# Attention block on one core: one of two integer adds goes from VectorE to GpSimd, a third PSUM bank for VectorE's tiles, and a changed planner

## The chip, the cores and the metric

The kernel runs on one core of one Trainium2 chip. The metric is device time in microseconds (us), the median of several executions. The engines are TensorE (PE), VectorE (DVE), ScalarE (ACT), GpSimd (POOL) and SyncE (SP), which issues most DMAs. Matmul results go to PSUM, in banks of 128 x 512 fp32.

## The reference

```python
# x (1, 2048, 448), wqkv (448, 1344), wo (448, 448), all bf16; 16 heads of 28
qkv = (x @ wqkv).reshape(B, S, 3, H, Dh).transpose(2, 0, 3, 1, 4)
q, k, v = qkv[0], qkv[1], qkv[2]
scores = jnp.einsum("bhqd,bhkd->bhqk", q, k) * (Dh ** -0.5)
p = softmax(scores, axis=-1)
o = jnp.einsum("bhqk,bhkd->bhqd", p, v)
return o.transpose(0, 2, 1, 3).reshape(B, S, D) @ wo
```

## The kernel before

The 16 heads form 4 groups of 4, and the 2048 queries form 4 blocks of 512. A group and a query block make a "set"; there are 16. In a set each of the 4 heads has 16 key tiles of 128 keys, so the whole run has 16 x 4 x 16 = 1024 score tiles of 128 keys x 512 queries. Scores are computed with keys on the partitions. A head uses 32 rows or columns of TensorE, so up to four heads' matmuls run side by side.

Each score tile must go through an exponential and then be multiplied with V. There are two ways:

- On ACT: `do_exp` (L802) takes a pair of tiles (128 x 1024, PSUM tag `a0` or `a1`) and writes `pt` in bf16, with its exact exponential.
- On VectorE: `do_a` (L817) converts one tile (128 x 512, PSUM tag `d0` or `d1`) into an int16 number `I` whose bits, read as bf16, approximate the exponential. Up to four tiles of one set make a "chain", kept side by side in one tile `I4` of 128 x 2048. The approximation is improved by using the chain three times with shifted exponents: `do_add` (L840) makes `J1 = I + 43` and `J2 = I + 85`, both 128 x 2048 int16 in SBUF, and the three are multiplied with V, V x 201/256 and V x 159/256 (tiles `VA`, `VS`), all into the same accumulator.

So a tile on ACT costs one output matmul on PE and a tile on VectorE costs three. `emit_s` (L621) issues the score matmuls; `do_pv` (L900) issues the output matmuls in waves of four heads, normally two waves in a row, into the PSUM bank `o`. The last column of V's tile is a one, so that the sums of the softmax come out with the output. At the end of a set `finish_set` copies `o` out, sends the sums through DMAs to get their reciprocals spread over the partitions, and multiplies.

Between these stand the "jobs" of PE: projections of K, Q and V for later groups (`k_job`, `q_job`, `v_job`, L230 and L445), bounds for the exponent (`kn_job`, `qn_job`), and the output projection (`oproj_job`, L481). They all use the PSUM bank `m`. Where PE has nothing to do, it multiplies zeros (`dense`, L651 and L654).

The order is made by a planner inside the kernel, while the program is built. It keeps an estimated time for each engine (`free`), a time for each event (`evt`) and for each PSUM bank (`res`), takes the engine that is free first and asks its `pick_...` function what to issue next. The estimated durations are constants such as `D_EXP = 0.912` for a pair on ACT. The estimates decide only the order: on the chip each engine works through its own list in that order and waits on semaphores for its inputs. `pick_pe` puts score matmuls first, then chooses between output matmuls and jobs; `dve_ok` decides whether another tile is given to VectorE, by comparing when the chain would be finished with when ACT would be; `d_banks` lists the banks that are free for such a tile; `pick_dve` orders conversions, adds and the other VectorE work. How many tiles go to ACT and how many to VectorE is therefore a result of the planning. `NCH = 3` chains may be open at once, and each of `I4`, `J1` and `J2` has three buffers.

GpSimd sets constants and loads `wo` at the start and does nothing after that.

Of the kernel before, what the change touches and what calls it, by code (L numbers as in the profile page):

```python
# [16 lines left out]
LAT = 0.2  # L17
# [4 lines left out]
D_EXP = 0.912  # L22
SLOW_V = 1.03
D_SOON = 0.0
S_LEAD = 0.44


class Op:
    def __init__(self, eng, dur, emit, need=(), gives=(), pri=0, acq=None, rel=None, gate=0, lag=0.0, land=0.0,
                 cols=0):  # L30
        self.eng, self.dur, self.emit = eng, dur * (SLOW_V if eng == "DVE" else 1.0), emit
        self.need, self.gives, self.pri = list(need), list(gives), pri
        self.acq, self.rel, self.gate, self.lag, self.land, self.cols = acq, rel, gate, lag, land, cols


@with_exitstack
def kernel(
# [135 lines left out]
        return psum.tile([P, QW], F32, name=tg, tag=tg, bufs=1)  # L173


    free = {"PE": 0.0, "ACT": 0.0, "DVE": 0.0, "SP": 0.0}
    evt = {}
    res = {"a0": 0.0, "a1": 0.0, "d0": 0.0, "d1": 0.0, "o": 0.0, "m": 0.0}
    ops = {"PE": [], "ACT": [], "DVE": [], "SP": []}
# [25 lines left out]
    def run(op, t):  # L205
        op.emit()
        if op.eng == "PE":
            note(t, op.cols)
        end = t + op.dur
        for n in op.gives:  # L210
# [35 lines left out]
    def k_job(g, sc, bank, pri, gate=0, split=2, eng="DVE", epri=None):  # L246
        key = ("K", g, sc)
        n = CC // split

        def mm(part):  # L250
            if part == 0:
                held[key] = bank_tile(bank) if bank[0] != "a" else pair_tile(bank)
            mm_proj(held[key][:, 0:QW], 1, g, sc, range(part * n, (part + 1) * n))

        def evac():
            KAt[(g, sc)] = big.tile([P, QW], BF16, name=f"KA{sc}", tag=f"KA{sc}", bufs=2)
            src = held[key][:, 0:QW]
# [13 lines left out]
        if g == 0:  # L271
            add("ACT", 0.5, lambda: act_square(key, kmask), need=[key + (split - 1,)],
                gives=[("ksq", g, sc)], rel=(bank, 2), pri=pri)
        else:
            add("DVE", 0.34, lambda: square(key, KAt[(g, sc)][:]), need=[key], gives=[("ksq", g, sc)], pri=pri)

    def kn_job(g, bank, pri, gate=0):
        key = ("KN", g)
# [24 lines left out]
        add("DVE", 0.65, spread_rows, need=[("kst", g)], gives=[("km", g)], pri=pri)  # L303

    def kn_first(sc, bank, pri):
        key = ("KN0", sc)
# [27 lines left out]
    def q_job(g, c, bank, pri, gate=0, split=2):  # L334
# [31 lines left out]
        if first:  # L366
            add("ACT", 0.5, lambda: act_square(key, qmask), need=[key + (split - 1,)], gives=[("qsq", g, c)],
                rel=(bank, 2), pri=pri)
        else:
            add("DVE", 0.34, lambda: square(key, QAt[(g, c)][:]), need=[key], gives=[("qsq", g, c)], pri=pri)  # L370
# [30 lines left out]
    def qn_job(g, cs, bank, pri, gate=0):  # L401
# [29 lines left out]
        add("DVE", 1.6, bound, need=[key + (len(cs) - 1,)], gives=[("su",) + key], rel=bank, pri=pri)  # L431
# [32 lines left out]
    def vs_job(h, b, pri):  # L464
# [4 lines left out]

        for k in range(1, NTERM):  # L470
            add("DVE", 0.335, lambda k=k: scale(k), need=[("V", h, XB * b), ("V", h, XB * b + 2)],
                gives=[("VS", h, b, k)], pri=pri + 0.1 * k)

    def oproj_job(c, tq, pri):
        key = ("O", c, tq)
# [185 lines left out]
    def dve_ok(t, k):  # L661
        if chain["cur"] is None and chain["used"] >= NCH:
            return False
        if chain["cur"] is not None and half_left(chain["cur"]["s"], 0) != half_left(chain["cur"]["s"], 1):
            return True
        fin = max(free["DVE"], t + 0.5) + 0.62 * (len(a_fifo) + k + 1) + 1.4 + (1.2 if adds else 0.0)
        return fin <= free["ACT"] + D_EXP * (len(exps) + max(0, left() // 2 - 2)) + 0.2

    def d_banks(t):
        return sorted((b for b in ("d0", "d1") if res[b] is not None and res[b] <= t + D_SOON), key=lambda b: res[b])  # L670

    def d_pick(s, t, acting, taken):
        ch = chain["cur"]
# [159 lines left out]
            chain["cur"] = None  # L833
            adds.append([ch, ch["n"], 1])

    def do_add(t):
        ch, m, k = adds[0]
        w = slice(0, m * QW)
        r = ch[k] = wk.tile([P, HG * QW], I16, name=f"J{k}", bufs=NCH)
        nc.vector.tensor_scalar(out=r[:, w], in0=ch["I"][:, w], scalar1=float(SHIFT[k]), scalar2=None, op0=ALU.add)  # L840
        end = t + (m * QW * 0.00026 + 0.068) * SLOW_V
        for n in range(m):
            pending.append({"step": ch["steps"][n], "k": k, "ap": r[:, n * QW:(n + 1) * QW].bitcast(BF16),
                            "ready": end + LAT, "pt": None, "ch": ch})
        adds[0][2] += 1
        if adds[0][2] == NTERM:
            adds.pop(0)
        return end

    def v_time(e):  # L850
        s, _, j = e["step"]
# [65 lines left out]
    def finish_set(s, end):  # L917
# [37 lines left out]
        add("DVE", 0.26, recip, need=[("den", s)], gives=[("rec", s)], pri=50)  # L955
        add("SP", 0.35, scatter, need=[("rec", s)], gives=[("scr", s)], land=1.1, pri=2)
        add("SP", 0.5, spread, need=[("scr", s)], gives=[("rr", s)], land=5.5, pri=2)
        add("DVE", 0.62, mul, need=[("rr", s)], gives=[("OT", g, c)], pri=60)

    def best(eng, t):  # L960
        b, nxt = None, None
        for op in ops[eng]:
            r = ready(op)
            if r is None:
                continue
            if r <= t:
                if b is None or op.pri < b.pri:
                    b = op
# [8 lines left out]
    def pick_pe(t):  # L977
# [24 lines left out]
            ws = ws[:1]  # L1002
            pv_ok = True
        op_ok = op is not None and t + op.dur <= dl + 0.1
        if pv_ok and (backlog >= 3 or last_chance or not op_ok):
            return do_pv(t, ws), None
        if op_ok:
            return run(op, t), None
# [22 lines left out]
    def pick_dve(t):  # L1031
        flush()
        op, nxt = best("DVE", t)
        if op is None or (op.pri >= 0 and op.gives[0][0] != "V"):
            if adds and adds[0][0]["s"] == cur["oset"] and not any(remain[cur["oset"]]):
                return do_add(t), None
            if a_fifo and a_fifo[0][0] <= t and a_fifo[0][3][0] == cur["oset"] \
                    and not any(remain[cur["oset"]]):
# [7 lines left out]
        if op is not None:  # L1046
            return run(op, t), None
        return None, nmin(nxt, a_fifo[0][0] if a_fifo else None)

    def pick_sp(t):  # L1050
        op, nxt = best("SP", t)
# [1 line left out]
            return run(op, t), None  # L1053
        return None, nxt

    pick = {"PE": pick_pe, "ACT": pick_act, "DVE": pick_dve, "SP": pick_sp}
    stuck = 0
    def late(op):
        return op.gives and op.gives[0][0] == "O" and op.gives[0][1] == CL - 1
# [1 line left out]
    while cur["oset"] < NSET or any(not late(op) for e in ops for op in ops[e]) or any(k[0] == "O" for k in held):  # L1061
# [11 lines left out]
        assert stuck < 4000, (t, cur, left(), pending, [(o.eng, o.need, o.acq) for q in ops.values() for o in q])  # L1073

    s = NSET - 1
    g, c = set_gc(s)
# [95 lines left out]
```

## Time and profile before

| | |
|---|---|
| time, median of 3 runs | 384.09 us (380.04 to 385.84) |
| the profiled execution's own time | 381.23 us |
| its span | 379.2 us |
| granted TensorE clock | 0.999 |
| busy: ACT, PE, DVE, POOL | 359.0, 346.4, 341.9, 20.0 us |
| exponential pairs on ACT | 376 |
| tiles converted on VectorE | 272 |
| adds on VectorE | 136 |
| matmuls of zeros in the program | 58 |

The profile is of one execution. "Busy" is the time in which an engine had an instruction running; for PE the ends of matmuls are modelled. In the lists of groups, a row gives line, engine, operation, output and input tiles, count, then busy time and the mean duration of one, and at last the idle time of the engine just before these instructions, with what ended it. Instructions of one engine overlap slightly, so the mean duration (1183 ns for an exponential pair) is more than busy time divided by count (919 ns). PEld is the loading of weights into TensorE.

### The profile page before, as it was taken

To read this page: it belongs to the slowest core of one execution; us is meant where nothing else is said; L and a number is where in the kernel's file an instruction comes from. 1 tells how busy PE (TensorE), PEld (TensorE's weight loads), DVE (VectorE), ACT (ScalarE), POOL (GpSimd) and SP (SyncE) were. 2 spreads that over 40 slices of the span, in tenths; PEclk is the share of its full clock that TensorE was granted. 3 is DMA by queue.
4 is the path that set the end of the run, shared out by engine and by line. 5 is a ranking of instruction groups with operands and counts; after the bars stand their busy time and mean duration, and the time that the engine had idled before them with its cause. 6 is when DMAs were issued, how large, how long until landed. Compare 5 with 4: busy or idle time off the path is not lost.

```text
span 379.2 us, 8747 instructions
## 1 busy us (share of the span) xinstructions
PE 346.4 (91%) x3442; PEld 113.3 (30%) x3462; DVE 341.9 (90%) x655; ACT 359.0 (95%) x400; POOL 20.0 (5%) x47
## 2 busy tenths in 40 slices
PE   7879999999999999999789999989889899989974
PEld 3443322222333233232222222222222222222222
DVE  2499998999999999999899899899999999999943
ACT  2779999999999999999999999999999999999992
POOL 8830000000000000000000000000000000000000
PEclk9999999999999999999999999999999999999999
DMA  8930001011100000011000001000000011110101
GB/s 251 246 102 16 3 19 38 3 41 28 41 6 15 18 3 29 14 28 40 4 30 7 25 15 41 28 31 2 28 5 4 28 39 42 37 43 12 56 14 48
DMA packets 16082, 14.03 MB, mean 37 GB/s; under 512 B 6077, under 2 KB 13609, under 8 KB 16041
## 3 DMA queue, kind: packets, MB, share of 16 engines
q1 hardware_dynamic: 13704, 11.18, 9.8%
q10 hardware_dynamic: 1824, 1.89, 1.8%
q8 instruction: 27, 0.44, 0.5%
q0 software_dynamic: 512, 0.40, 0.5%
q14 instruction: 15, 0.11, 0.1%
HBM read 7.37 MB, written 1.96 MB: 25 GB/s over the span
## 4 chain that ended last, share of the span: by engine, by line
ACT 56%; PE 22%; issue 9%; DMA 6%; DVE 4%; SPq 2%; ACTq 0%; DVEq 0%
ACT pt L802 54%; PE a L621 9%; PE o L900 6%; PE m L230 3%; DMA rr<-scr 3%; PE m L445 2%; DMA WRAW<-in_wqkv_dram 2%; SPq L359 2%; DVE I L817 1%; DMA QP<-zero 1%; DVE QA L353 1%; DVE J L840 1%; DMA den<-o_sb 1%; ACT sq L244 0%; ACT XT L517 0%
## 5 line engine op out<-in xcount | busy, mean ns | idle before, releaser
L802 ACT ACTIVATE pt<-a 128x1024 bf16<-128x1024 f32 x376 | 345.6, 1183 | 1.5 <-PE d L621 1.1
L817 DVE TENSOR_SCALAR I<-d 128x512 int16<-128x512 f32 x272 | 180.0, 682 | 8.0 <-PE d L621 6.6
L621 PE MATMUL a<-QP,KA 32*128 32x512 bf16 (+1 forms) x742 | 144.9, 380 | 18.2 <-ACT pt L802 17.0
L900 PE MATMUL o<-pt,VA 128*32 128x512 bf16 x752 | 106.5, 385 | 0.5 <-ACT pt L802 0.5
L621 PEld LDWEIGHTS <-KA 32*128 32x128 bf16 (+1 forms) x1024 | 52.6, 91 | 155.8 <-issue 153.6
L621 PE MATMUL d<-QP,KA 32*128 32x512 bf16 x267 | 92.6, 384 | 0.2 <-DVE I L817 0.2
L840 DVE TENSOR_SCALAR J<-I 128x2048 int16<-128x2048 int16 x136 | 90.1, 684 | 0.4
L900 PE MATMUL o<-J,VS 128*32 128x512 bf16 x544 | 74.4, 385 | 0.3
L900 PE MATMUL o<-I,VA 128*32 128x512 bf16 x272 | 65.9, 385 | 0.6 <-issue 0.5
L230 PE MATMUL m<-XT,WRAW 112*32 112x512 bf16 x464 | 35.5, 384 | 0.5 <-ACT XT L517 0.3
L900 PEld LDWEIGHTS <-VA 128*32 128x32 bf16 x1024 | 23.9, 94 | 37.0 <-issue 36.7
L900 PEld LDWEIGHTS <-VS 128*32 128x32 bf16 x544 | 16.5, 94 | 16.4 <-issue 16.4
L445 PE MATMUL m<-WRAW,XT 112*128 112x224 bf16 x112 | 15.4, 261 | 0.0
L230 PEld LDWEIGHTS <-WRAW 112*32 112x32 bf16 x512 | 8.4, 94 | 16.0 <-issue 12.9
L445 PEld LDWEIGHTS <-XT 112*128 112x128 bf16 x128 | 10.2, 97 | 7.8 <-issue 6.3
L262 DVE TENSOR_SCALAR KA<-m,kmask,ones 128x512 bf16<-128x512 f32 x13 | 10.4, 803 | 2.1 <-ACT sq L244 1.9
L353 DVE TENSOR_SCALAR QA<-m,qmask 128x512 bf16<-128x512 f32 x15 | 11.1, 742 | 0.5 <-PE m L230 0.5
L515 DVE COPY XT<-a 112x1024 bf16<-112x1024 bf16 x4 | 2.8, 692 | 9.4 <-ACT XT L517 7.8
L651 PE MATMUL o<-zero 128*128 128x512 bf16 x29 | 10.0, 384 | 1.3 <-issue 1.3
L481 PE MATMUL m<-WO,xs 128*128 128x448 bf16 x36 | 11.0, 359 | 0.0
L951 DVE TENSOR_TENSOR xs<-o_sb,rr 128x512 bf16<-128x512 f32 x12 | 8.2, 683 | 2.5 <-DMA rr<-scr 2.5
L929 DVE COPY o_sb<-o 128x512 f32<-128x512 f32 x15 | 10.3, 685 | 0.1
(104 smaller groups left out, 155.0 us busy)
## 6 DMA issues: line engine op xcount, KB each, us to landing
rr<-scr SPq DMA_DIRECT2D x15, 256.0 KB
QP<-zero SPq DMA_DIRECT2D x16, 128.0 KB
QP<-QA SPq DMA_DIRECT2D x60, 28.0 KB
out_dram<-osb SPq DMA_DIRECT2D x14, 112.0 KB
xs<-in_x_dram SPq DMA_DIRECT2D x3, 448.0 KB
WRAW<-in_wqkv_dram ACTq DMA_DIRECT2D x3, 392.0 KB
QP<-su SPq DMA_DIRECT2D x30, 2.0 KB
xs<-in_x_dram ACTq DMA_DIRECT2D x1, 448.0 KB
```

Source lines behind the costliest of these rows:

```text
L230: nc.tensor.matmul(out=ps[HP * i:HP * (i + 1), :], lhsT=WRAW[t][:, cc, h * Dh:h * Dh + HP], rhs=XT[c][:, cc, :], start=(cc == 0), stop=(cc ...
L262: nc.vector.tensor_scalar(out=KAt[(g, sc)][:], in0=src, scalar1=kmask[:, 0:1], scalar2=ones[:, 0:1], op0=ALU.mult, op1=ALU.add)
L353: nc.vector.tensor_scalar(out=t[:], in0=held[key][:, 0:QW], scalar1=qmask[:, 0:1], scalar2=None, op0=ALU.mult)
L445: nc.tensor.matmul(out=held[key][:, part * w:(part + 1) * w], lhsT=XT[b][:, cc, t * P:(t + 1) * P], rhs=WRAW[2][:, cc, h * w:(h + 1) * w], ...
L481: nc.tensor.matmul(out=held[key][:, 0:D], lhsT=otile(g, c)[:, tq * P:(tq + 1) * P], rhs=WO[:, g, :], start=(g == 0), stop=(g == G - 1))
L621: nc.tensor.matmul(out=out_ap, lhsT=KAt[(g, j // XB)][r, (j % XB) * P:(j % XB + 1) * P], rhs=q[r, :], start=True, stop=True, tile_position ...
L651: nc.tensor.matmul(out=cur["o"][:], lhsT=zero[:, 0:P], rhs=zero[:], start=False, stop=False, skip_group_check=True)
L802: nc.scalar.activation(out=pt[:], in_=ps[:], func=ACT.Exp, scale=LN2 / 128.0)
L817: nc.vector.tensor_scalar(out=dst, in0=pd[:], scalar1=BIAS, scalar2=0.0, op0=ALU.add, op1=ALU.max)
L840: nc.vector.tensor_scalar(out=r[:, w], in0=ch["I"][:, w], scalar1=float(SHIFT[k]), scalar2=None, op0=ALU.add)
L900: nc.tensor.matmul(out=o[HP * i:HP * (i + 1), :], lhsT=vt[:, gg, j % XB, HP * i:HP * (i + 1)], rhs=e["ap"], start=(SETMM[key] == 1), stop= ...
L929: nc.vector.tensor_copy(out=st["o_sb"][:], in_=o[:])
```

## The change

- Of the two adds of a chain, VectorE now makes only `J2 = I + 85`; GpSimd makes `J1 = J2 - 42`, from VectorE's result.
- The planner has a GpSimd engine, with a duration of 2.3 us for such an add (`D_POOL`), and a notion of a port shared by VectorE and GpSimd: VectorE operations marked `port=True`, and its adds, are not planned while a GpSimd add is planned to run, and a GpSimd add is not planned while one of these is.
- `d_banks` may offer the bank `m` as a third bank for a VectorE tile, when fewer than two of `d0` and `d1` are free, fewer than two tiles wait for conversion and no job is about to need `m`.
- `dve_ok` reckons 3.5 us instead of 1.4 us from the last conversion to the end of a chain.
- `pick_pe` lets a job with a priority value below 40 go ahead of waiting output matmuls; `pick_dve` puts adds ahead of conversions; the planner's clock is advanced differently when an engine finds nothing to do.

The diff, cut to its core (the added parameter `port=True` on seven operations with SBUF inputs is left out after the first):

```diff
+D_POOL = 2.3
...
-    free = {"PE": 0.0, "ACT": 0.0, "DVE": 0.0, "SP": 0.0}
+    free = {"PE": 0.0, "ACT": 0.0, "DVE": 0.0, "SP": 0.0, "POOL": 0.0}
     evt = {}
+    port = {"DVE": 0.0, "POOL": 0.0}
+    pool_q = []
...
-            add("DVE", 0.34, lambda: square(key, KAt[(g, sc)][:]), need=[key], gives=[("ksq", g, sc)], pri=pri)
+            add("DVE", 0.34, lambda: square(key, KAt[(g, sc)][:]), need=[key], gives=[("ksq", g, sc)], pri=pri, port=True)
...
-        fin = max(free["DVE"], t + 0.5) + 0.62 * (len(a_fifo) + k + 1) + 1.4 + (1.2 if adds else 0.0)
+        fin = max(free["DVE"], t + 0.5) + 0.62 * (len(a_fifo) + k + 1) + 0.7 + D_POOL + 0.5 + (1.2 if adds else 0.0)
...
     def d_banks(t):
-        return sorted((b for b in ("d0", "d1") if res[b] is not None and res[b] <= t + D_SOON), key=lambda b: res[b])
+        out_ = sorted((b for b in ("d0", "d1") if res[b] is not None and res[b] <= t + D_SOON), key=lambda b: res[b])
+        if len(out_) < 2 and res["m"] is not None and res["m"] <= t and len(a_fifo) < 2:
+            soon = [ready(op) for op in ops["PE"] if op.acq == "m"]
+            if not any(r is not None and r <= t + 1.0 for r in soon):
+                out_.append("m")
+        return out_
...
-    def do_add(t):
-        ch, m, k = adds[0]
+    def add_term(eng, ch, m, k, src, shift, end):
         w = slice(0, m * QW)
         r = ch[k] = wk.tile([P, HG * QW], I16, name=f"J{k}", bufs=NCH)
-        nc.vector.tensor_scalar(out=r[:, w], in0=ch["I"][:, w], scalar1=float(SHIFT[k]), scalar2=None, op0=ALU.add)
-        end = t + (m * QW * 0.00026 + 0.068) * SLOW_V
+        eng.tensor_scalar(out=r[:, w], in0=src[:, w], scalar1=float(shift), scalar2=None, op0=ALU.add)
         for n in range(m):
             pending.append({"step": ch["steps"][n], "k": k, "ap": r[:, n * QW:(n + 1) * QW].bitcast(BF16),
                             "ready": end + LAT, "pt": None, "ch": ch})
-        adds[0][2] += 1
-        if adds[0][2] == NTERM:
-            adds.pop(0)
         return end
 
+    def do_add(t):
+        ch, m, _ = adds.pop(0)
+        end = port["DVE"] = t + (m * QW * 0.00026 + 0.068) * SLOW_V
+        pool_q.append((end + LAT, ch, m))
+        return add_term(nc.vector, ch, m, 2, ch["I"], SHIFT[2], end)
+
+    def pick_pool(t):
+        if not pool_q:
+            return None, None
+        if pool_q[0][0] > t:
+            return None, pool_q[0][0]
+        if port["DVE"] > t:
+            return None, port["DVE"]
+        _, ch, m = pool_q.pop(0)
+        end = port["POOL"] = t + D_POOL * m / HG
+        return add_term(nc.gpsimd, ch, m, 1, ch[2], SHIFT[1] - SHIFT[2], end), None
...
+            if op.port:
+                r = max(r, port["POOL"])
...
-        if pv_ok and (backlog >= 3 or last_chance or not op_ok):
+        if pv_ok and (backlog >= 3 or last_chance or not op_ok) and not (op_ok and op.pri < 40 and pts_used[0] < NPT):
             return do_pv(t, ws), None
...
     def pick_dve(t):
         flush()
         op, nxt = best("DVE", t)
+        can_add = adds and port["POOL"] <= t
+        can_a = a_fifo and a_fifo[0][0] <= t
...
-        if a_fifo and a_fifo[0][0] <= t:
+        if can_add:
+            return do_add(t), None
+        if can_a:
             return do_a(t), None
-        if adds:
-            return do_add(t), None
...
-        cand = nmin(nxt, others if others > t else None)
-        free[e] = max(t + 0.02, cand if cand is not None else t + 0.05)
+        free[e] = max(t + 0.02, nmin(nxt, others))
```

More of the change, by code (lines that the diff above doesn't have):

```diff
@@ L29, in __init__ @@
     def __init__(self, eng, dur, emit, need=(), gives=(), pri=0, acq=None, rel=None, gate=0, lag=0.0, land=0.0,
-                 cols=0):
+                 cols=0, port=False):
         self.eng, self.dur, self.emit = eng, dur * (SLOW_V if eng == "DVE" else 1.0), emit
         self.need, self.gives, self.pri = list(need), list(gives), pri
-        self.acq, self.rel, self.gate, self.lag, self.land, self.cols = acq, rel, gate, lag, land, cols
+        self.acq, self.rel, self.gate, self.lag, self.land, self.cols, self.port = acq, rel, gate, lag, land, cols, port
 @with_exitstack
@@ L173, in bank_tile @@
         return psum.tile([P, QW], F32, name=tg, tag=tg, bufs=1)
-    free = {"PE": 0.0, "ACT": 0.0, "DVE": 0.0, "SP": 0.0}
+    free = {"PE": 0.0, "ACT": 0.0, "DVE": 0.0, "SP": 0.0, "POOL": 0.0}
     evt = {}
+    port = {"DVE": 0.0, "POOL": 0.0}
+    pool_q = []
     res = {"a0": 0.0, "a1": 0.0, "d0": 0.0, "d1": 0.0, "o": 0.0, "m": 0.0}
-    ops = {"PE": [], "ACT": [], "DVE": [], "SP": []}
+    ops = {"PE": [], "ACT": [], "DVE": [], "SP": [], "POOL": []}
     cnt = {"step": 0, "half": 0}
@@ L209, in run @@
         end = t + op.dur
+        if op.port:
+            port["DVE"] = end
         for n in op.gives:
@@ L302, in kn_job @@
         add("DVE", 0.61, red, need=[("KNp", g, NQC - 1)], gives=[("kst", g)], rel=bank, pri=pri)
-        add("DVE", 0.65, spread_rows, need=[("kst", g)], gives=[("km", g)], pri=pri)
+        add("DVE", 0.65, spread_rows, need=[("kst", g)], gives=[("km", g)], pri=pri, port=True)
     def kn_first(sc, bank, pri):
@@ L369, in q_job @@
         else:
-            add("DVE", 0.34, lambda: square(key, QAt[(g, c)][:]), need=[key], gives=[("qsq", g, c)], pri=pri)
+            add("DVE", 0.34, lambda: square(key, QAt[(g, c)][:]), need=[key], gives=[("qsq", g, c)], pri=pri, port=True)
             add("SP", 2.4, rows, need=[key, ("QZ", c, g % 2)] + ([("Oset", ORDER.index((g - 2, c)))] if g > 1 else []),
@@ L430, in qn_job @@
                 acq=bank if k == 0 else None)
-        add("DVE", 1.6, bound, need=[key + (len(cs) - 1,)], gives=[("su",) + key], rel=bank, pri=pri)
+        add("DVE", 1.6, bound, need=[key + (len(cs) - 1,)], gives=[("su",) + key], rel=bank, pri=pri, port=True)
         add("SP", 1.2 * len(cs), place, need=[("su",) + key] + [("QR", g, c) for c in cs],
@@ L471, in vs_job @@
             add("DVE", 0.335, lambda k=k: scale(k), need=[("V", h, XB * b), ("V", h, XB * b + 2)],
-                gives=[("VS", h, b, k)], pri=pri + 0.1 * k)
+                gives=[("VS", h, b, k)], pri=pri + 0.1 * k, port=True)
     def oproj_job(c, tq, pri):
@@ L954, in finish_set @@
         add("SP", 0.6, gather, need=[("osb", s)], gives=[("den", s)], land=1.5, pri=2)
-        add("DVE", 0.26, recip, need=[("den", s)], gives=[("rec", s)], pri=50)
+        add("DVE", 0.26, recip, need=[("den", s)], gives=[("rec", s)], pri=50, port=True)
         add("SP", 0.35, scatter, need=[("rec", s)], gives=[("scr", s)], land=1.1, pri=2)
         add("SP", 0.5, spread, need=[("scr", s)], gives=[("rr", s)], land=5.5, pri=2)
-        add("DVE", 0.62, mul, need=[("rr", s)], gives=[("OT", g, c)], pri=60)
+        add("DVE", 0.62, mul, need=[("rr", s)], gives=[("OT", g, c)], pri=60, port=True)
     def best(eng, t):
@@ L965, in best @@
                 continue
+            if op.port:
+                r = max(r, port["POOL"])
             if r <= t:
@@ L1033, in pick_dve @@
         op, nxt = best("DVE", t)
+        can_add = adds and port["POOL"] <= t
+        can_a = a_fifo and a_fifo[0][0] <= t
         if op is None or (op.pri >= 0 and op.gives[0][0] != "V"):
-            if adds and adds[0][0]["s"] == cur["oset"] and not any(remain[cur["oset"]]):
+            last = not any(remain[cur["oset"]]) if cur["oset"] < NSET else False
+            if can_add and last and adds[0][0]["s"] == cur["oset"]:
                 return do_add(t), None
-            if a_fifo and a_fifo[0][0] <= t and a_fifo[0][3][0] == cur["oset"] \
-                    and not any(remain[cur["oset"]]):
+            if can_a and last and a_fifo[0][3][0] == cur["oset"]:
                 return do_a(t), None
@@ L1041, in pick_dve @@
             return run(op, t), None
-        if a_fifo and a_fifo[0][0] <= t:
+        if can_add:
+            return do_add(t), None
+        if can_a:
             return do_a(t), None
-        if adds:
-            return do_add(t), None
-        if op is not None:
-            return run(op, t), None
-        return None, nmin(nxt, a_fifo[0][0] if a_fifo else None)
+        return None, nmin(nxt, a_fifo[0][0] if a_fifo else None, port["POOL"] if adds else None)
     def pick_sp(t):
@@ L1054, in pick_sp @@
         return None, nxt
-    pick = {"PE": pick_pe, "ACT": pick_act, "DVE": pick_dve, "SP": pick_sp}
+    pick = {"PE": pick_pe, "ACT": pick_act, "DVE": pick_dve, "SP": pick_sp, "POOL": pick_pool}
     stuck = 0
@@ L1069 @@
         others = min(free[n] for n in free if n != e)
-        cand = nmin(nxt, others if others > t else None)
-        free[e] = max(t + 0.02, cand if cand is not None else t + 0.05)
+        free[e] = max(t + 0.02, nmin(nxt, others))
         stuck += 1
-        assert stuck < 4000, (t, cur, left(), pending, [(o.eng, o.need, o.acq) for q in ops.values() for o in q])
+        assert stuck < 40000, (t, cur, left(), pending, [(o.eng, o.need, o.acq) for q in ops.values() for o in q])
     s = NSET - 1
```

## The prediction

> **What bounds the kernel now.** I read the page's busy shares first, then the costliest groups, then each engine's waits, then timelines for the cadence. The page:
>
> ```profile
> span 379.2 us, 8747 instructions
> PE 346.4 (91%) x3442; PEld 113.3 (30%) x3462; DVE 341.9 (90%) x655; ACT 359.0 (95%) x400; POOL 20.0 (5%) x47
> ...
> ACT  2779999999999999999999999999999999999992
> POOL 8830000000000000000000000000000000000000
> ...
> L802 ACT ACTIVATE pt<-a 128x1024 bf16<-128x1024 f32 x376 | 345.6, 1183 | 1.5 <-PE d L621 1.1
> L817 DVE TENSOR_SCALAR I<-d 128x512 int16<-128x512 f32 x272 | 180.0, 682 | 8.0 <-PE d L621 6.6
> L621 PE MATMUL a<-QP,KA 32*128 32x512 bf16 (+1 forms) x742 | 144.9, 380 | 18.2 <-ACT pt L802 17.0
> ...
> L840 DVE TENSOR_SCALAR J<-I 128x2048 int16<-128x2048 int16 x136 | 90.1, 684 | 0.4
> ```
>
> Three engines are above 90%, so the share alone decides nothing. The idle column does. ACT makes 376 exponential pairs (two 128x512 tiles each) and in the whole run waited 1.5 us before them. PE waited 17.0 us for ACT ahead of its score matmuls; VectorE waited 6.6 us for scores. ACT is saturated from 22.8 us (its first exponential in the timeline) until about 369.7 us, and PE and VectorE, though nearly full, follow it. So only fewer exponentials on ACT shorten the main stage: 345.6 / 376 = 0.919 us for each pair taken away. GpSimd (POOL) has nothing after 23.6 us.
>
> **Parts of the change.** I set the instruction lists of the two programs side by side, engine by engine, in program order. Counts before and after:
>
> - ACT: exponential pairs 376 to 364, all else equal. 12 x 0.919 = **-11.0 us** on the engine that sets the end.
> - VectorE: tiles in its own exponential 272 to 296 (265 from the d banks, 31 from the projections' bank m); adds 136 to 74. At 0.662 us each (180.0 / 272 and 90.1 / 136): 24 x 0.662 - 62 x 0.662 = -25.2 us, so 341.9 becomes 316.7, some 86% of the new span. Off the path: nothing from here, but more room.
> - PE: each VectorE tile enters the output product three times instead of once, so 48 matmuls more (pt 752 to 728, I 272 to 296, J 544 to 592). They run four abreast; two waves of four stand 361.83 to 362.37 in the timeline, 0.54 us with the switch, so 12 waves are 2.6 us (0.22 each) to 3.2 (0.27). 18 zero matmuls that only fill gaps go, 0.32 each (257.07 to 257.39): -5.8 us. PE's cover for the shorter span is its 17.0 us of waiting for ACT: 17.0 - 11.0 - 3.2 + 5.8 = 8.6 us are left, plus 40 fillers. Cost nothing; if that cover were gone, a late PE would go to ACT one for one.
> - GpSimd: 74 adds of 128x2048 int16, SBUF to SBUF, each reading the first add's result. The trace has no such operation. The nearest rows:
>
> ```profile
> 1.01 0.29 POOL L133 TENSOR_SCALAR_AFFINE_SELECT ident<-ident 128x128 bf16<-128x128 bf16 x1
> ...
> 3.49 1.03 POOL L161 MEMSET VA<- 128x1024 bf16 x1
> ...
> 11.51 1.67 POOL L163 MEMSET WO<- 128x1792 bf16 x1
> ```
>
> The select reads and writes 128 elements in 287 ns, against 185 ns for one of 128x1: 0.80 ns an element, and 185 + 2047 x 0.80 = 1.83 us for 2048. The memsets, which only write, give (1671 - 1017) / 768 = 0.85 ns, and 1671 + 256 x 0.85 = 1.89 us. If reading and writing each took the memset's rate, one after the other: 1.89 + 2048 x 0.85 = 3.63 us. So 1.83 to 3.63; I take 1.9, as the select both reads and writes at the low rate. As work, 74 x 3.63 = 269 us would still fit; what counts is delay.
>
> The delay: a chain is four tiles, then the first add on VectorE, then GpSimd's, then PE. A product placed too early in PE's fixed order blocks the next score matmuls behind it, and ACT waits for those. From the order I counted, for each of the 74 chains, the score pairs that PE issues between the chain's last tile and its first product with GpSimd's result: 4 pairs in 2 chains, 5 in 12, 6 in 22, 7 in 16, 8 in 17, 9 in 5. A pair lasts 0.911 us (15 exponentials in 13.93 us at 249.18, the last one 1.18 long). The available time is pairs x 0.911 + 0.33 for the score group ahead of the product. The needed time is 0.39 (score) + 0.69 (tile) + 0.60 for each VectorE instruction between (0 to 4, counted chain by chain) + 0.68 (add) + three hand-overs of 0.1 + GpSimd's add. VectorE's 0.60 cadence is read here:
>
> ```profile
> 104.32 0.68 DVE L840 TENSOR_SCALAR J<-I 128x2048 int16<-128x2048 int16 x1
> 104.91 0.68 DVE L817 TENSOR_SCALAR I<-d 128x512 int16<-128x512 f32 x1
> 105.52 0.68 DVE L951 TENSOR_TENSOR xs<-o_sb,rr 128x512 bf16<-128x512 f32 x1
> ```
>
> Lateness summed over the chains by the add's duration: none at 1.89 us (median margin 1.85), 1.0 us in all at 2.3, 4.2 at 2.83, 12.2 at 3.2, 26.0 at 3.64. One VectorE instruction queued ahead of the last tile adds 0.60 to each chain; 1.89 + 0.60 = 2.49 gives 1.9 us. I take **+1.5 us** for the new wait.
>
> The buffers: GpSimd's add also waits on PE for the buffer used three chains earlier. Chains come every 364 / 74 = 4.9 pairs, so three of them are 13.4 us, and the last product stands at most 12 pairs (10.9 us) behind its chain's last tile. Nothing there.
>
> Starting up: GpSimd's memsets and weight DMAs end at 23.6 us, and VectorE's first tile conversion starts at 22.97. The first add cannot precede four of them, so it is not queued behind the start. SP's queue has the same 174 instructions in kind and number. Tail: the last chain's scores stand at pair 359 of 364, which leaves 5 pairs (4.6 us) against 0.39 + 0.69 + 0.68 + 0.3 + 1.9 = 4.0; the 9.5 us from the last exponential to the end stay.
>
> The m bank for 31 tiles: each holds it for a score, a tile and two hand-overs, 0.39 + 0.69 + 0.2 = 1.28 us. Counted in score pairs, 29 of them stand at pairs 166 to 190 and 237 to 298; the projections before them end at pairs 159 and 231 and the next begin at 191 and 301. So these tiles use the bank where nothing else does: nothing. If all 31 stood in a projection's way, 31 x 1.28 = 40 us of bank time would be to place, of which only what an exponential waits for would count.
>
> Between the two engines: do they disturb each other? VectorE's four PSUM copies at 8.11, 10.71, 11.67 (beside GpSimd memsets) and 13.68 (beside none) all took 0.69 us. So an operation that reads PSUM is not held by a GpSimd write. The tile conversions read PSUM too. What reads and writes SBUF on VectorE shows no overlap with GpSimd here; 15 such instructions (three reciprocals, two squares, two scalings of V and eight small steps) stand within three places behind a first add in the new order. Each could wait up to 1.9 us. I take 0 for them, since the margin above (median 1.85) covers most, and keep 15 x (1.9 - 1.25) = 9.8 us as the other end, 1.25 being the median margin at 2.49.
>
> The Trainium skill, in "SBUF — State Buffer", section "Who interferes with whom", speaks against the change: a VectorE instruction that reads two SBUF tensors, or uses both its ports, and a GpSimd instruction exclude each other for their whole length, while one with a PSUM source is free of it. By that rule the PSUM rows agree and the 15 would wait. The skill's "GPSIMD Engine Reference", section "Elementwise — side-by-side cycle accounting", gives about 1.8 cycles an element for a tight loop; by it the add would be an estimated 3.1 us, just short of the point where rival 2 below begins, and the sum some 380 us.
>
> **Sum.** 381.23 (the profiled execution; span 379.2 and 2.0 around it) - 11.0 + 1.5 = 371.7. That execution is 2.9 below the median of 384.09 of the runs shown (380.04 to 385.84), which would become 374.6. I say **372.5**.
>
> **Rivals.**
> 1. The gain is eaten. The 15 blocked VectorE instructions pass on the 9.8 us above: 372.5 + 9.8 = **382**, between 376 and 386. For it: PE's cover falls to 8.6 us. Against: reciprocals, squares and bounds prepare a later set, and no product waits for them within a few pairs.
> 2. GpSimd's add is slow: **slower than before**. Mechanism: PE stands at the product with GpSimd's tile, the scores behind it are late, ACT idles. Place: every chain in the main stage. It decides from the point where lateness passes 11.0 us, at an add of about 3.15 us. At 3.63 it costs 26: 381.23 - 11.0 + 26 = **396**. For it: int16 in and out with an fp32 addend is more than a select does. Against: the select's 0.80 ns.
> 3. GpSimd's adds hold VectorE altogether, conversions too: 74 x 1.9 = 141 us on top of 316.7, more than the span, and VectorE (with 37 us idle as now) sets the end at about **495**. Against: the 0.69 us copies.
> 4. The change does not do what it says: excluded by the counts.
>
> **Chances.** Forecast 0.62 (range of its own 368 to 376), rival 1 0.21, rival 2 0.14, rival 3 0.03. Two per cent (7.7 us, about what a measurement of this kernel tells from no change) puts faster at 0.62, within at 0.22 (rival 1 and a little of rival 2), slower at 0.16 (the rest). The range runs from 367.5 (the lowest run shown, 380.04, less 11.0 is 369.0, and 1.5 less for their scatter of 5.8 us) to 387, past the end of rival 1; about 0.15 lies above and 0.04 below.
>
> **What would show it.** Right: exponential pairs x364 with about 334 us busy and idle before them below 5 us; GpSimd adds near 1.9 us, 140 us in all; VectorE near 317 us; PE's wait for ACT near 9 us. Wrong in the delay step: PE's products from J waiting for POOL by more than 5 us, and ACT waiting as long. Wrong in the sharing step: VectorE's adds, squares or reciprocals longer than now (0.68, 0.41, 0.24) or conversions beyond 0.68. Wrong in the sum: pairs at another cadence than 0.919.

## The result, and the profile after

The changed kernel takes 533.26 us (median of 4 runs, 531.68 to 534.50) against 382.06 for the kernel before: a ratio of 1.398, 95% interval 1.386 to 1.410. The forecast was 372.5 us, faster. Direction and size are wrong, and the time lies above the price of every rival too. Some executions of one kernel run some 2% longer at a lower granted clock, and the medians below leave these out.

The page of the changed kernel, cut to the lines that answer those shown of before:

```profile
span 530.6 us, 8950 instructions
PE 407.3 (77%) x3475; PEld 107.6 (20%) x3492; DVE 437.2 (82%) x617; ACT 365.0 (69%) x388; POOL 417.5 (79%) x121
...
ACT  3778777766858677786667687667475657876681
POOL 8676687784868766787888867888888988888881
PEclk9989998877979789885868898867685668988898
...
L849 POOL TENSOR_SCALAR J<-J 128x2048 int16<-128x2048 int16 x74 | 397.4, 5371 | 98.6 <-DVE J L849 65.0
L812 ACT ACTIVATE pt<-a 128x1024 bf16<-128x1024 f32 x364 | 351.7, 1033 | 143.6 <-PE d L626 72.7
L827 DVE TENSOR_SCALAR I<-d 128x512 int16<-128x512 f32 x265 | 175.4, 681 | 42.8 <-PE d L626 39.9
L922 PE MATMUL o<-J,VS 128*32 128x512 bf16 x592 | 109.7, 454 | 89.1 <-POOL J L849 85.9
...
L849 DVE TENSOR_SCALAR J<-I 128x2048 int16<-128x2048 int16 x74 | 116.5, 1576 | 3.4 <-DVE I L827 0.5
```

Read them in this order. The counts are as forecast: 364 pairs, 74 adds on each of the two engines. ACT, which waited 1.5 us before, now waits 143.6 us. Its pairs with their waiting take 351.7 + 143.6 = 495.3 us, 148.2 more than the 347.1 of before; the span grew by 151.4. So nearly the whole loss is ACT standing idle, and it waits for PE's scores.

PE in turn waited 85.9 us for POOL, at the products with GpSimd's result. And GpSimd's add takes 5.37 us, where the prediction took 1.9 and bounded it at 3.63. Where its 74 adds stand in the run (durations: least, median, most in ns; then the first and last start in us):

```profile
L849 POOL TENSOR_SCALAR J<-J x74: 5362/5366/5665, 27.8 to 514.1; 128x2048 int16<-128x2048 int16 x74
```

The first starts at 27.8 us, so 74 adds of this length cannot end before 27.8 + 397.4 = 425 us, in whatever order. That alone is more than the 372.5 us of the forecast and the 382 us of the kernel before. The waits come on top: from the first add to the end of the last, 491.7 us, GpSimd stood idle for 94 us.

Two other lines are off. VectorE's own add grew from 684 to 1576 ns, while the conversions, which read PSUM, stayed at 681. And the clock that PE is granted is 0.835 on average, where it was 0.999.

One place shows both waits. The timelines of GpSimd, VectorE and PE from 205 us (start, duration, engine):

```profile
205.06 5.37 POOL L849 TENSOR_SCALAR J<-J 128x2048 int16<-128x2048 int16 x1 [3.55 <-DVE J L849]
...
208.03 2.94 DVE L849 TENSOR_SCALAR J<-I 128x2048 int16<-128x2048 int16 x1
210.93 0.69 DVE L951 COPY o_sb<-o 128x512 f32<-128x512 f32 x1
...
210.48 0.40 PE L922 MATMUL o<-J,VS 128*32 128x512 bf16 x4 [3.00 <-POOL J L849]
210.81 0.39 PE L626 MATMUL a<-QP,KA 32*128 32x512 bf16 x2
```

GpSimd's add ends at 210.43. PE stood 3.00 us at its product, and the next score matmuls came right behind it. VectorE's next add began at 208.03 and ended 2.94 us later, 0.54 us after GpSimd's: it too was held.

So there are two suspects that share one root, the long add, and two more that the change brings along:

- A: PE waits for an add that is too long.
- B: the long add keeps VectorE's SBUF operations from the port, and the chains come late.
- C: the new order, the m bank or the mended planner is bad in itself.
- D: the slower PE clock.

### The profile page after: what moved, and what is told of

Same layout as the page of the kernel before. It is cut to its first block, busy times and chain, and to the rows that moved or that the text cites. A ratio compares the mean times of both kernels' runs of the same rounds, so it can differ in the third digit from the quotient of the medians.

```text
span 530.6 us, 8950 instructions
## 1 busy us (share of the span) xinstructions
PE 407.3 (77%) x3475; PEld 107.6 (20%) x3492; DVE 437.2 (82%) x617; ACT 365.0 (69%) x388; POOL 417.5 (79%) x121
## 3 DMA queue, kind: packets, MB, share of 16 engines
q10 hardware_dynamic: 1824, 1.89, 1.2%
## 4 chain that ended last, share of the span: by engine, by line
DVE 32%; POOL 32%; PE 26%; issue 5%; DMA 3%; POOLq 1%; SPq 0%; ACT 0%; DVEq 0%; ACTq 0%
POOL J L849 32%; PE o L922 11%; DVE J L849 10%; DVE I L827 9%; PE a L626 8%; DVE VS L471 3%; DMA WRAW<-in_wqkv_dram 2%; PE m L235 2%; DVE su L421 2%; DVE xs L973 2%; DVE sq L245 1%; PE m L450 1%; POOLq L1190 1%; DVE QA L358 1%; DVE VA L461 1%
## 5 line engine op out<-in xcount | busy, mean ns | idle before, releaser
L849 POOL TENSOR_SCALAR J<-J 128x2048 int16<-128x2048 int16 x74 | 397.4, 5371 | 98.6 <-DVE J L849 65.0
L812 ACT ACTIVATE pt<-a 128x1024 bf16<-128x1024 f32 x364 | 351.7, 1033 | 143.6 <-PE d L626 72.7
L922 PE MATMUL o<-J,VS 128*32 128x512 bf16 x592 | 109.7, 454 | 89.1 <-POOL J L849 85.9
L626 PE MATMUL a<-QP,KA 32*128 32x512 bf16 (+1 forms) x718 | 160.6, 447 | 6.6 <-ACT pt L812 4.8
L922 PE MATMUL o<-pt,VA 128*32 128x512 bf16 x728 | 133.4, 452 | 0.0
L849 DVE TENSOR_SCALAR J<-I 128x2048 int16<-128x2048 int16 x74 | 116.5, 1576 | 3.4 <-DVE I L827 0.5
L922 PE MATMUL o<-I,VA 128*32 128x512 bf16 x296 | 86.7, 473 | 0.7 <-issue 0.3
L626 PEld LDWEIGHTS <-KA 32*128 32x128 bf16 (+1 forms) x1024 | 39.4, 93 | 174.8 <-issue 172.4
L827 DVE TENSOR_SCALAR I<-m 128x512 int16<-128x512 f32 x31 | 21.1, 679 | 3.7 <-PE m L626 3.7
L471 DVE TENSOR_SCALAR VS<-VA 128x1024 bf16<-128x1024 bf16 x16 | 20.0, 1287 | 0.0
L626 PE MATMUL m<-QP,KA 32*128 32x512 bf16 x31 | 15.5, 499 | 0.0
L245 DVE TENSOR_TENSOR sq<-QA 128x512 bf16<-128x512 bf16 x15 | 14.0, 935 | 0.0
```

Of the source, the lines that this page charges most:

```text
L245: nc.vector.tensor_tensor(out=t[:], in0=src, in1=src, op=ALU.mult)
L471: nc.vector.tensor_scalar(out=VS[k - 1][h][b][:].rearrange("p g t e -> p (g t e)"), in0=VA[h][b][:].rearrange("p g t e -> p (g t e)"), sca ...
L626: nc.tensor.matmul(out=out_ap, lhsT=KAt[(g, j // XB)][r, (j % XB) * P:(j % XB + 1) * P], rhs=q[r, :], start=True, stop=True, tile_position ...
L812: nc.scalar.activation(out=pt[:], in_=ps[:], func=ACT.Exp, scale=LN2 / 128.0)
L827: nc.vector.tensor_scalar(out=dst, in0=pd[:], scalar1=BIAS, scalar2=0.0, op0=ALU.add, op1=ALU.max)
L849: eng.tensor_scalar(out=r[:, w], in0=src[:, w], scalar1=float(shift), scalar2=None, op0=ALU.add)
```

## The experiments

### The price of the add by itself

> A kernel of unit prices alone: the attention is left out and the output is zeros. GpSimd first makes adds and copies of 128 to 2048 columns in int16, bf16 and fp32 with nothing beside them; then six int16 adds of 2048 columns and eight memsets run while VectorE alternates conversions from PSUM, int16 adds in SBUF and a product of two SBUF tiles. If the 5.37 us of the changed kernel is the add's own price, the lone 2048-column add takes 5.3 to 5.4 us here and a 704-column one would take about 1.9; if the 5.37 us comes from sharing with VectorE, the lone one takes 1.9 to 3.6. If the two engines exclude each other for an instruction's length, VectorE's SBUF adds (0.68 us alone) grow to up to 6 us beside GpSimd's adds and its conversions from PSUM stay at 0.68; if they share a rate instead, both grow by a common share.

The groups of the probe, GpSimd with nothing beside it, and then the first GpSimd add that runs beside VectorE:

```profile
L63 POOL TENSOR_SCALAR b<-a 128x2048 f32<-128x2048 f32 x1 | 5.4, 5368 | 0.0
L63 POOL TENSOR_SCALAR bbf<-abf 128x2048 bf16<-128x2048 bf16 x1 | 5.4, 5367 | 0.0
L63 POOL TENSOR_SCALAR b<-a 128x2048 int16<-128x2048 int16 x1 | 5.4, 5363 | 0.1
L73 POOL TENSOR_TENSOR bbf<-abf 128x2048 bf16<-128x2048 bf16 x1 | 3.6, 3597 | 0.1
L63 POOL TENSOR_SCALAR b<-a 128x1024 int16<-128x1024 int16 x1 | 2.8, 2768 | 0.1
L71 POOL COPY b<-a 128x2048 int16<-128x2048 int16 x1 | 1.9, 1893 | 0.0
```

The 5.37 us are the add's own price, without any neighbour: (5363 - 2768) / 1024 = 2.53 ns a column, in int16, bf16 and fp32 alike. A copy of the same size, which also reads and writes, takes 1.89 us, what the prediction took for the add. So reading and writing cost what it thought; an add of a constant costs 3.5 us more. An add of two tensors (one bf16 tile with itself) takes 3.60, less than an add of a constant.

```profile
45.15 5.37 POOL L63 TENSOR_SCALAR h<-g 128x2048 int16<-128x2048 int16 x1
45.21 5.33 DVE L78 COPY s<-sync 128x8 f32<-128x8 f32 x1 [41.40 <-POOL sync L76]
```

VectorE's copy of 8 columns, SBUF to SBUF, that started 0.06 us after GpSimd's add took 5.33 us: until that add ended. For this copy it is exclusion for the instruction's length and not a shared rate. It agrees with the Trainium skill, "SBUF — State Buffer", section "Who interferes with whom": whoever starts first holds the port for the whole instruction. The conversions from PSUM kept running beside the adds (0.67 to 0.69 us each, but for the first, recorded at 1.82, which was queued behind the held copy).

The hold is not the same for every operation. A VectorE product of two SBUF tiles in the changed kernel, beside a GpSimd add:

```profile
196.14 5.37 POOL L849 TENSOR_SCALAR J<-J 128x2048 int16<-128x2048 int16 x1 [2.89 <-DVE kbc L297]
196.46 3.86 DVE L973 TENSOR_TENSOR xs<-o_sb,rr 128x512 bf16<-128x512 f32 x1
```

It ended at 200.32, 1.19 us before GpSimd's add (201.51). Its own work takes 0.68, so it was let go 1.87 us before that end. All held products and squares of this run behave so, and one that starts more than 3.5 us into a GpSimd add takes its usual time. Here the trace differs from the rule quoted above.

### Without GpSimd, same order

```diff
-        return add_term(nc.gpsimd, ch, m, 1, ch[2], SHIFT[1] - SHIFT[2], end), None
+        return add_term(nc.vector, ch, m, 1, ch[2], SHIFT[1] - SHIFT[2], end), None
```

> The changed kernel's plan and order throughout, but the second add is issued on VectorE at the place where it was planned for GpSimd. Theory A (GpSimd's add is too long, and PE waits for it) and theory B (GpSimd holds the port and VectorE waits) both expect 372 to 388 us: 364 pairs on ACT, VectorE at 316.7 + 74 x 0.66 = 366 us busy. Theory C (the new order or the m bank is bad in itself) expects over 450 us.

This run, e1, took 390.72 us, 1.021 of before (1.013 to 1.029): just above the 372 to 388 that A and B gave, far from C. VectorE was busy 361.8 us (366 expected), and ACT waited 14.3 us for scores. The order is not what costs 150 us; C falls.

### A short add, same order and same waits

```diff
-        w = slice(0, m * QW)
+        w = slice(0, m * QW if k == 2 else 704)
...
-            ... "ap": r[:, n * QW:(n + 1) * QW].bitcast(BF16),
+            ... "ap": r[:, (n * QW if k == 2 else 0):((n + 1) * QW if k == 2 else QW)].bitcast(BF16),
```

> The changed kernel in the same order, but GpSimd adds only the first 704 of the 2048 columns, and all four tiles of a chain are multiplied from the first 512 of them, so three of four second terms are wrong; every wait between the engines stays. At 2.6 ns a column the add takes about 1.9 us, the duration that the prediction took. Theory A expects 370 to 378 us, 364 pairs busy 334 us and ACT idle before them below 5 us. Theory B expects a loss left in proportion to the shorter hold, 116 x 1.9 / 5.4 = 40 us of VectorE time, and 376 to 400 us. Theory C expects over 450 us.

This run, e2, took 369.54 us, 0.964 of before (0.954 to 0.973). Its groups:

```profile
L812 ACT ACTIVATE pt<-a 128x1024 bf16<-128x1024 f32 x364 | 334.4, 1150 | 1.1 <-PE d L626 1.0
L849 POOL TENSOR_SCALAR J<-J 128x704 int16<-128x704 int16 x74 | 146.2, 1975 | 188.3 <-DVE J L849 126.4
...
L849 DVE TENSOR_SCALAR J<-I 128x2048 int16<-128x2048 int16 x74 | 50.8, 687 | 3.4 <-DVE I L827 0.5
```

With an add of 1.98 us everything else in the prediction is there: pairs busy 334.4 us (about 334 expected), ACT's waiting 1.1 us, VectorE busy 322.8 (317 expected), its adds unheld at 687 ns. In place of the 40 us of holds that B expected in proportion there is almost nothing; the order was planned with 2.3 us for the add. The length of this one instruction decides whether the change gains or loses.

### PE no longer waits for GpSimd; the port is still held

```diff
-            ... "ap": r[:, n * QW:(n + 1) * QW].bitcast(BF16),
+            ... "ap": ch[2][:, n * QW:(n + 1) * QW].bitcast(BF16),
```

> The changed kernel in the same order with GpSimd's full add, but PE multiplies the first add's result in both places, so nothing on PE waits for GpSimd; the second term is wrong by that. GpSimd still reads the first add's buffer and holds the port. Theory A (PE's wait) expects the time to fall to 375 to 400 us, or to what GpSimd's own length sets, 28 + 74 x 5.37 = 425 us at most 445, because the first add's buffers are freed by GpSimd. Theory B (the port) expects it to stay at 480 to 530 us with VectorE's adds still at 1.5 us on average.

This run, e6, took 507.07 us; the profile is of a run of 517.38. Both lie in B's range, and above the 445 us that the expectation gave as the most if only GpSimd's own length were left. So A is not needed for most of the loss. VectorE's adds now take 1844 ns:

```profile
L849 POOL TENSOR_SCALAR J<-J 128x2048 int16<-128x2048 int16 x74 | 397.5, 5372 | 87.5 <-DVE J L849 85.6
L812 ACT ACTIVATE pt<-a 128x1024 bf16<-128x1024 f32 x364 | 350.7, 1036 | 130.7 <-PE d L626 82.8
...
L849 DVE TENSOR_SCALAR J<-I 128x2048 int16<-128x2048 int16 x74 | 136.4, 1844 | 3.4 <-DVE I L827 0.5
```

GpSimd and VectorE take turns: VectorE's add must get past GpSimd's, and GpSimd's next add needs VectorE's. 74 x (5.37 + 0.68) = 448 us for that alone, with some 28 us ahead of the first. The changed kernel itself does the same: in both traces VectorE's add ended after GpSimd's previous add in 72 of 73 cases, and GpSimd's median pause between two adds was 0.63 us here and 0.70 there (2.39 with the short add of e2).

### PE's wait without the long hold

GpSimd adds 704 columns and then makes tiny operations one after the other until the length of the wait is reached; PE's product waits for the last.

```diff
-        eng.tensor_scalar(out=r[:, w], in0=src[:, w], scalar1=float(shift), scalar2=None, op0=ALU.add)
+            eng.tensor_scalar(out=r[:, 0:704], in0=src[:, 0:704], scalar1=float(shift), scalar2=None, op0=ALU.add)
+            for _ in range(15):      # 9 in the second kernel
+                eng.tensor_scalar(out=tick[:], in0=tick[:], scalar1=1.0, scalar2=None, op0=ALU.add)
+            eng.tensor_scalar(out=r[:, 0:64], in0=tick[:, 0:1].to_broadcast([P, 64]), scalar1=float(shift), ...)
```

> The changed kernel in the same order, but GpSimd adds 704 columns, then makes 15 tiny operations of 4 columns and a last one of 64 columns that PE's product waits for; the second terms are wrong. PE's wait is about as long as in the changed kernel (5 to 6 us after the first add), the port is held in one piece for 2 us and then only in pieces of some 0.1 to 0.2 us. Theory A (PE's wait alone is enough): 131 us of summed lateness by the prediction's own formula at 5.4 us, 470 to 510 us. Theory B (the port hold is needed): 372 to 410 us.

This run, e10, took 626.84 us. It missed its own aim: a tiny operation came every 0.335 us and the chain's work on GpSimd was 7.5 us, so 74 of them alone fill 554 us. The second one was sized anew:

> As e10, with 9 tiny operations instead of 15, which made GpSimd's work per chain 7.6 us there (1.98 + 15 x 0.335 + 0.39); with 9 it is 5.4 us, the length in the changed kernel, while the port is held in one piece for 2 us only. The second terms are wrong. Theory A (PE's wait is enough alone): 470 to 530 us with VectorE's adds at 0.69 us. Theory B (a loss needs the port hold): 372 to 410 us.

It, e10b, took 513.04 us, with VectorE's adds at 689 ns and PE waiting 88.6 us for GpSimd:

```profile
L814 ACT ACTIVATE pt<-a 128x1024 bf16<-128x1024 f32 x364 | 349.7, 1037 | 127.7 <-PE d L628 67.0 <-PE a L628 50.3 <-PE m L628 8.2
L857 DVE TENSOR_SCALAR J<-I 128x2048 int16<-128x2048 int16 x74 | 50.9, 689 | 3.4 <-POOL tick L854 0.5
```

So a large loss does not need the holds of B either. The prediction's formula for the summed lateness gives some 131 us at 5.37 us, and 381.23 - 11.0 + 131 = 501 us: 12 us below what was measured. That is not a clean test of the formula, which lets every chain find GpSimd free. Here GpSimd's work was 5.6 us a chain, 416 us in all, and in 50 of 73 cases VectorE's add was done while GpSimd was still at the chain before.

A's run and B's run both leave GpSimd's long work in place, and with it a bound of 425 us or more. Each brings the time above 507 us, and together they give 533: the two losses do not add. How much of the 151 us is want of time on GpSimd, how much PE's wait and how much VectorE's holds, no run separates.

### The clock

```diff
+            for _ in range(8):      # ahead of the first product of each GpSimd add
+                nc.tensor.matmul(out=cur["o"][:], lhsT=zero[:, 0:P], rhs=zero[:], start=False, stop=False, ...)
```

> The changed kernel in the same order, but before the first product that waits for a GpSimd add PE multiplies eight zero tiles (8 x 0.22 = 1.7 us at full clock, 592 in all), so that it does not stand idle for so long. If the granted clock of 0.835 is a cause of its own, the clock rises above 0.9 and the time falls by 20 to 60 us. If the slow clock only follows from idling while GpSimd and VectorE set the pace, the clock rises and the time stays at 515 to 540 us.

536.46 us with the clock at 0.972 instead of 0.835:

```profile
L920 PE MATMUL o<-zero 128*128 128x512 bf16 x550 | 136.7, 390 | 6.5 <-issue 6.2
```

The zeros filled PE's waiting (14.8 us left of the 85.9) and the granted clock rose, yet the time stayed. So a clock near full speed does not win the loss back in this order. But the zeros took 136.7 us of PE's time, more than the 71 us of waiting that they filled; PE's other work shrank from 407.3 to 340.9 us. A gain from the clock and the price of the zeros could cancel, so a small part for D stays open. With a short add the clock was 0.994 (e2) without these zeros.

### Telling the planner the truth

```diff
-D_POOL = 2.3
+D_POOL = 5.5
```

> The changed kernel with one number changed: the planner reckons 5.5 us for GpSimd's add instead of 2.3, and makes a new order with 391 pairs on ACT and 242 tiles on VectorE. GpSimd's add stays 5.37 us. Theories A and B: the waits vanish, because the order leaves room for them, and what remains is 15 pairs more than before, 384 + 15 x 0.919 = 394 to 402 us. Theory C (m bank and the rest of the planner): over 450 us.

This run, e3, took 544.78 us, slower still. I expected A and B to vanish here, and they did not. The timeline shows one reason, VectorE and GpSimd at 301 us:

```profile
301.58 0.68 DVE L973 TENSOR_TENSOR xs<-o_sb,rr 128x512 bf16<-128x512 f32 x1
302.18 5.34 DVE L297 COPY kbc<-kst 128x32 f32<-128x32 f32 x1
...
301.82 5.67 POOL L849 TENSOR_SCALAR J<-J 128x2048 int16<-128x2048 int16 x1 [1.05 <-DVE J L849]
```

In the plan both VectorE operations come before GpSimd's add, since the planner lets VectorE pick again before a waiting GpSimd. On the chip GpSimd got the port between them, and a copy of 32 columns was held for 5.34 us. In the mean VectorE's 61 adds took 1618 ns. The second try reserves the port from the moment that the first add ends:

```diff
+        port["POOL"] = end + LAT + D_POOL * m / HG
         pool_q.append((end + LAT, ch, m))
...
-        if port["DVE"] > t:
-            return None, port["DVE"]
```

> As e3 (the planner reckons 5.5 us), and the port is reserved for GpSimd in the plan from the end of VectorE's add: no VectorE operation that needs it is planned until GpSimd's add is over. The order has 398 pairs on ACT, 228 tiles on VectorE. In e3 GpSimd's add began on the chip between two such VectorE operations that the plan had back to back ahead of it, and the second was held 5.34 us. If that is why e3 did not recover, the waits go and 22 pairs more than before remain: 384 + 22 x 0.919 = 402 to 415 us, VectorE's adds near 0.69 us. If the long add hurts in another way, over 480 us.

This run, e11, took 450.76 us: 94 us less than before the port was reserved, but the 402 to 415 that I expected were not reached. VectorE's adds still averaged 1102 ns. ACT's waiting is another one now:

```profile
L812 ACT ACTIVATE pt<-a 128x1024 bf16<-128x1024 f32 x398 | 367.9, 1111 | 45.1 <-PE o L921 39.4
```

ACT waits 39.4 us, at 13 places, for PE's products to free its `pt` buffers. In e3 this wait was 80.6 us of 140.3. At the place I looked at (313.5 to 317.4 us) a set was ending: `o` was copied out at 315.98, and ACT went on at 317.44. That all 13 are ends of sets that wait for their last long add was not tried. With 398 pairs (22 more than before) and 45 us of waiting the sum is 382.4 + 20.2 + 43.6 = 446 us.

### What is the rest of the change worth?

The new planner and the m bank, both adds on VectorE:

```diff
-        pool_q.append((end + LAT, ch, m))
-        return add_term(nc.vector, ch, m, 2, ch["I"], SHIFT[2], end)
+        add_term(nc.vector, ch, m, 2, ch["I"], SHIFT[2], t + one)
+        return add_term(nc.vector, ch, m, 1, ch["I"], SHIFT[1], t + 2 * one)
```

> The changed kernel's planner and m bank with both adds on VectorE and GpSimd out of the loop, planned so: 379 pairs, 266 tiles and 134 adds on VectorE. If the m bank and the mended planner are worth something without GpSimd, below 380 us; if the gain of e9 needs the work taken off VectorE, 3 pairs more than before at 0.919, 384 to 391 us.

384.14 us, 1.005 of before (1.0005 to 1.010), with 379 pairs. Three pairs more at 0.919 would be 2.8 us, 0.7%. Without GpSimd the rest of the change shows no gain.

### A version that beats both

Two int16 numbers are added as one int32, so that GpSimd has 1024 columns; and an add of two tensors (here the second is one column, read again for each) is the cheaper form:

```diff
+    shiftc = const.tile([P, 1], I32, name="shiftc")
+    nc.gpsimd.memset(shiftc[:], (SHIFT[1] - SHIFT[2]) * 65537)
...
+            h = m * QW // 2
+            eng.tensor_tensor(out=r[:].bitcast(I32)[:, 0:h], in0=src[:].bitcast(I32)[:, 0:h],
+                              in1=shiftc[:].to_broadcast([P, h]), op=ALU.add)
```

> The changed kernel in the same order, but GpSimd's add takes two int16 numbers as one int32: 1024 columns, a product of the form tensor + tensor with a constant -42 in both halves (no borrow, since every number is at least 85). The lone tensor + tensor add of 2048 columns took 3.60 us, so 1024 should take about 1.85 us. If the length of GpSimd's add is the whole cause (theory A or B alike), 367 to 376 us, like the 704-column add with its 370; if the form of the instruction matters beyond its length, over 390.

Two executions of this run, e9, took 372.13 and 373.41 us, against 379.98 to 385.28 for the kernel before beside it. Then with the port reserved and the planner told 2.1 us:

> The packed int32 add of e9 (1.90 us), the planner told 2.1 us, with the port reserved as in e11; 364 pairs. ACT idle before its pairs was 4.9 us in e9 and VectorE's products with two SBUF inputs were 0.80 instead of 0.68 us. If the rest of those holds goes, 368 to 374 us and 0.96 to 0.97 of the kernel before; if the plan loses as much by reserving, the same as e9.

This run, e12, took 370.11 us, 0.970 of before (0.965 to 0.975), the best of the kernels that compute everything:

```profile
L814 ACT ACTIVATE pt<-a 128x1024 bf16<-128x1024 f32 x364 | 334.8, 1160 | 3.2 <-PE d L628 2.8
L853 POOL TENSOR_TENSOR J<-J,shiftc 128x1024 int32<-128x1024 int32 x74 | 140.3, 1896 | 195.9 <-DVE J L856 140.1
```

GpSimd's add takes 1.90 us and ACT waits 3.2 us. With an add of this length the change gains about what was forecast.

## Why the prediction was wrong

- **What bounds the kernel, and the sum's first term** held: where ACT was kept fed (e2, e12) 364 pairs took 334 to 335 us, 11 less than 376 did, and the time fell by 12 to 14 us.
- **The failed step is the duration of GpSimd's add**, "1.83 to 3.63; I take 1.9". It measured 5.37 us. The select and the memsets priced the columns' reading and writing, and a copy does cost that (1.89). The arithmetic of an add with a constant was taken as free. The upper bound, "one after the other", was built from the same rows and could not see it. Everything that the prediction said of the rest of the path was worked out with this duration, and came true when the add was made short (e2, e12).
- **The Trainium skill's 1.8 cycles** ("GPSIMD Engine Reference", "Elementwise — side-by-side cycle accounting") gave 3.1 us, nearer than my choice but still too short; 2.53 ns a column is about 3 cycles by the 1.2 GHz that the same page states. The measurement decides.
- **"As work, 74 x 3.63 = 269 us would still fit; what counts is delay"** fell with it: at 5.37 us the work is 397 us, and from 27.8 us on it cannot end before 425. The delay comes on top.
- **The lateness formula**, fed with the right duration, comes near (501 us against 513 for the wait alone), but it leaves out that GpSimd may still be at the chain before, so this is in part luck. Rival 2 named the mechanism and its place; its price of 396 us and its chance of 0.14 came from the bound of 3.63. Its threshold of 3.15 us was not tried: no run lies between 1.98 and 5.37 us.
- **"I take 0" for sharing the port** failed for the long add: 15 instructions within three places behind an add were counted, but a 5.37 us hold covers nine VectorE instructions (at 0.60 each) and the next chain's add. VectorE's adds, squares, scalings, bounds and products with two SBUF inputs grew by some 110 us in all (the adds alone by 116.5 - 50.6 = 66). For a short add the step was right, and the reciprocals among the 15 were not held even beside the long one (0.24 us). Rival 3 (conversions held too) is refuted: they stayed at 0.68 us.
- **The m bank, the tail, the buffers and PE's cover** cost nothing, as said (e2).

## What to carry to other kernels

Before work moves to another engine, the price of that very instruction must be measured or its bound must be open: rows of other operations on the same engine price the memory traffic, not the arithmetic, and here the add cost 2.8 times the copy. Then multiply: the price times the count, from the first start on, is a bound that no order can beat, and here it lay above the forecast. In an order that is fixed in advance, an underestimated duration is not paid once but at each place where another engine waits behind it. And where two engines exclude each other, the order planned between them counts only if the chip cannot take another.

## What the runs showed of the hardware

- GpSimd over 2048 columns: copy 1.89 us, add of two tensors 3.60 (bf16), add of a constant 5.37, the last the same in int16, bf16 and fp32; the add of two int32 tensors over 1024 columns takes 1.90. So two int16 numbers packed into an int32, in the form with two tensors, are added 2.8 times as fast as with the constant. Packing with a constant was not run.
- VectorE's copies, adds and scalings from SBUF to SBUF wait for the end of a GpSimd add, even when they are small: 8 columns took 5.33 us. Its products and squares of two SBUF tiles are held too, but only until 1.9 us before that end. Not held were its reciprocals (0.24 us), its conversions from PSUM (0.68) and an operation on a single column (0.15, `km`, in e3). At the place shown, GpSimd got its turn between two VectorE operations that follow each other without a gap.
- PE's mean granted clock was 0.835 with PE waiting 85.9 us for GpSimd, and 0.972 with zero matmuls put into the waits, at the same time of the kernel.
